# All four chunks run their second and third PV back to back, with LayerNorm of the next chunk ahead of the pair

## Chip, cores and metric

One core of a Trainium2 chip runs the kernel. The metric is the device time of one execution in microseconds (us); three executions of the kernel before took 562.66, 563.76 and 564.58 us, the median is 563.76. The engines are TensorE (PE), VectorE (DVE), ScalarE (ACT), GpSimd (POOL) and SyncE (SP), which here only issues transfers (DMA).

## What is computed

A transformer block whose two halves stand side by side on one normalised input: attention with 32 heads of 18 and a sliding window of 256 keys, and a gated feed-forward. The sequence is S = 2048, the width D = 576, the hidden width F = 4608, all in bf16.

```python
xn = _layernorm(x)                       # no weights
q, k, v = split(xn @ wqkv)               # 32 heads of 18
scores = einsum("bhqd,bhkd->bhqk", q, k) * 18 ** -0.5
p = softmax(where(0 <= i - j < 256, scores, -1e9))
attn = (p @ v) @ wo
ffn = (silu(xn @ w1) * (xn @ w3)) @ w2
return x + attn + ffn
```

## The kernel before

**Chunks and phases.** The sequence is cut into four chunks of 512 tokens (`c` = 0 to 3), each of four tiles of 128. A chunk has three phases on TensorE. First come the projections (L449; chunk 0 has its own ahead of the loop). Then follow 36 *units* (`u`, loop at L999): a unit is 128 columns of the hidden layer, nine pairs of matmuls of 64 rows each (`unit_pairs`, L701), one pair for gate and up each time; its tanh runs on ScalarE (`unit_tanh`, L710), its two multiplications on VectorE (`unit_h`, L716 and L719). The last phase, called P2 in the code, multiplies by W2 and Wo (L761, L767), adds the residual and stores.

**Attention between the units.** While the units run, attention is fed in between their matmul pairs. Heads go in eight groups of four (`g`). A *score step* (`scores` L575, `exps` L584, `masks` L611) makes one P tile; a group has four steps in chunk 0 and five in the others, so 32 and 40 steps a chunk. A *PV* (`pv`, L632) multiplies the P tiles of two groups by V: PV `j` takes groups 2j and 2j+1, so a chunk has four, of 72 small matmuls in chunk 0 and 96 in the others. PV 3 runs as P2 begins. PV 0 to 2 run among the units: each alone, after a unit (L1049), or two as a pair without anything between them, in the middle of a unit (L1009). `JOINT` says which two and where.

**After a PV.** VectorE moves the two PSUM banks of its result out (`pv_out`, L641) and takes a reciprocal (`o_scale`, L646), GpSimd scales (L647), VectorE turns the result back (`o_turn`, L654) into the buffer `od[j % 2]`, of which there are two, and transfers put its rows into `oT` (`o_pack` and `o_rest`, L658). `o_rest`, for the rows of PV 0 alone, is seven small transfers over the following units, on SP's queue, in chunk 0 on ScalarE's. A pair needs two more places for `pv_out`: they are P tiles that the pair has just read (`kept`).

**PSUM.** Eight banks: two for scores (`SC`), and three pairs (`JOBS`) which units and PVs take in turn. A unit can start only when VectorE has read what its pair held three jobs ago; a PV takes a pair like a unit does.

**P tiles.** They lie in ten buffers of their own (`pt`) and in memory that is free for a while: the last eight rows of `hT` (`h`), `stage` (`sh`), `od`, and the four W2 buffers (`w2`). `early` lists where the first steps' tiles go, `free` is the list from which later steps take, `held` keeps two for group 6, and `release` gives a PV's tiles back. A step waits in the order until a tile is to be had.

**The order** is written by the loop itself with a clock that counts matmul pairs: `last` says by when the steps should be done, and `spaced_step` spreads them over what remains, at least 7.5 pairs apart. A PV may run 20 pairs after its last step (`PV_AFTER`). Engines take their instructions in this order, SP its transfers too, each behind its waits.

**LayerNorm of the next chunk.** `near` gives for each of the next chunk's four tiles three units: one for the statistics (`ln_stats`, L357 to L360 on VectorE, L365 and L367 on GpSimd), one for the normalisation (`ln_apply`, L382 on VectorE) and one for the transfer that transposes it into `xnT` (`xn_send`, L407 on SP). The fourth tile has 34, 35 and 40 (the last one in P2). The tiles themselves come by `load_x` (L298): chunk 1's first two in unit 6 of chunk 0, the third in unit 8 and the fourth in unit 17 of each chunk. Weights of the units come in parts through SP (`load_part`, L322), W2 in pieces into a ring of four buffers (`load_w2`, L349), the first four of a chunk while its units still run.

Before, `JOINT` gave chunks 1 and 3 the pair of PV 1 and 2 in unit 27, and chunk 2 the pair of PV 0 and 1 in unit 18 with PV 2 alone after unit 25. Chunk 0 had no pair: its PVs ran after units 14, 20 and 27.

Of the kernel before, what the change touches and what calls it, by code (L numbers as in the profile page):

```python
# [164 lines left out]
def bass_parallel_sum__sliding_block__glu_gated_swiglu__prompt_kernel(  # L165
# [18 lines left out]
    NC = S // CH  # L184
# [13 lines left out]
    with ExitStack() as es:  # L198
# [143 lines left out]
        def load_w2(upto):  # L342
            nonlocal n2fill
            if n2fill >= min(upto, NC * 2 * NFC):
                return
            s = n2fill % NW2
            half, fc = divmod(n2fill % (2 * NFC), NFC)
            n2fill += 1
            add("sp", lambda e: e.dma_start(  # L349
                w2[s][:], B_w2[fc * 512:(fc + 1) * 512, half * HD:(half + 1) * HD].rearrange("(fl p) d -> p fl d", p=128)),  # L350
                w=[("w2", s)], dma=f"w2_{s}")
# [398 lines left out]
        def p2_item(c, item, xs):  # L750
            nonlocal of_ctr
            what, half, fc, k, tt, sl, last = item
            if what == "rest":
                wo_rest(half, False, k)
                return
            d0 = half * HD
            bank = PS[:, ACC[tt], 0:HD]
            key = [("ps", ACC[tt])]
            if what == "w2":
                f = fc * 4 + k  # L760
                add("pe", lambda e: e.matmul(  # L761
                    bank, hT[:, f, tt * 128:(tt + 1) * 128], w2[sl][:, k, :], start=(f == 0 and half == 1), stop=False),
                    r=[("h", f), ("w2", sl)], **{"w" if f == 0 and half == 1 else "j": key})
                if last:
                    load_w2((c + 1) * 2 * NFC + (2 if c + 1 < NC and JOINT[c + 1][0] == 0 else 0))
            elif what == "wo":
                add("pe", lambda e: e.matmul(  # L767
                    bank, oT[:, k, tt * 128:(tt + 1) * 128], wo[:, k, d0:d0 + HD], start=False, stop=(k == 3 and (half == 0 or c + 1 == NC))),
                    r=[("oT", j) for j in range(G // 2)] + ["wo"], j=key)
            else:  # L770
                o = of_ctr % NOF
                of_ctr += 1
                t = c * TB + tt
                add("dve", lambda e: e.tensor_tensor(ofin[:, o, :], bank, xp[xs[tt]][:, d0:d0 + HD], ALU.add),  # L774
                    r=key + [("xp", xs[tt])], w=[("of", o)])
                add("sp", lambda e: e.dma_start(out2[t * 128:(t + 1) * 128, d0:d0 + HD], ofin[:, o, :]),
                    r=[("of", o)], dma=f"out{o}")
# [132 lines left out]
        span_main(2, G, "act", slice(0, 2))  # L910

        PV_COST, PV_AFTER = 6.6, 20
        JOINT = {1: (1, 27, 7), 2: (0, 18, 4), 3: (1, 27, 8)}

        for c in range(NC):
            NS = len(steps_of(c))
            att = [(g, s) for g in range(G) for s in range(NS)]
            near = {0: (20, 22, 23), 1: (24, 26, 27), 2: (30, 32, 33), 3: (34, 35, 40)}
            plan = near if c + 1 < NC else {}
            stat, apply, xt = ({v[k]: i for i, v in plan.items()} for k in range(3))  # L920
            loads = {8: (2,), 17: (3,)} if c + 1 < NC else {}
# [3 lines left out]
            if c:  # L925
                total += 9 * sum(COST[kind] for kind, _ in PROJ)
            start = 60 if c == 0 else 42
            last = total - 24
            nxt = soon = start
            clock = 0.0  # L930
            done = 0
            pv_ready = {}
            free = [("pt", n) for n in range(NPT)]
            if c:
                free += [("sh", n) for n in range(4 if JOINT[c][0] == 0 else 2)]
            early = [("h", n) for n in range(4)]
            if c:
                early += [("w2", (c * 2 * NFC + n) % NW2) for n in range(2 if JOINT[c][0] == 0 else 0, 4)] + [("od", n) for n in range(NOD)]
            held = {} if c == 0 or JOINT[c][0] == 0 else {6 * NS: ("sh", 2), 6 * NS + 1: ("sh", 3)}
            side = {}  # L940
            jobs = {}
            next_pv = 0
# [1 line left out]
            def later(u, what):  # L944
                side.setdefault(u, []).append(what)

            def release(j, kept):
                for g in (2 * j, 2 * j + 1):
                    for st in range(NS):
                        sl = pt_of[(c, g, st)]  # L950
                        ok = ("pt", "sh", "h", "w2") if c and at_u < 22 and JOINT[c][0] == 1 else ("pt", "sh")
                        if sl[0] in ok:
                            (kept if kept is not None and len(kept) < 2 and sl[0] in ("pt", "sh") else free).append(sl)

# [44 lines left out]
            for u in range(NF):  # L999
# [6 lines left out]
                b0 = jobs[u] = job()  # L1006
                for n in range(9):
                    into = nxt - (clock + 9 - n)
                    if c and (u, n) == JOINT[c][1:]:  # L1009
                        ja = JOINT[c][0]  # L1010
                        assert next_pv == ja and ja + 1 in pv_ready and clock >= pv_ready[ja + 1], (c, next_pv, clock, pv_ready)
                        two = [job(), job()]
                        job_ctr += 1
                        kept = []
                        _DEBUG.setdefault("joint", []).append((c, u, n, done, round(clock - pv_ready[ja + 1], 1), len([o for o in P.ops if o.eng == "pe"])))
                        for m, j in enumerate((ja, ja + 1)):
                            pv(c, j, two[m])
                            clock += PV_COST
                            release(j, kept)
                        next_pv = ja + 2  # L1020
                        for m, sl in enumerate(kept):
                            uqs[2 + m:] = [pt_slot(sl).rearrange("p q r -> p (q r)").bitcast(dt.float32)]
                            uq_keys[2 + m:] = [pt_keys(sl)]
                        pv_out(two[0][0], 0)
                        pv_out(two[0][1], 1)
                        o_scale(0)
                        pv_out(two[1][0], 2)
                        pv_out(two[1][1], 3)
                        g = 2 * ja
                        later(u, lambda g=g: (o_turn(g, 0), o_turn(g, 1), o_scale(1)))  # L1030
                        later(u + 1, lambda g=g: o_turn(g + 1, 0))
                        later(u + 2, lambda g=g, ja=ja: (o_turn(g + 1, 1), o_pack(ja, "sp"), o_scale(2)))
                        later(u + 3, lambda g=g: (o_turn(g + 2, 0), o_turn(g + 2, 1), o_scale(3)))
                        later(u + 3, lambda kept=kept: free.extend(kept))
                        later(u + 4, lambda g=g: o_turn(g + 3, 0))
                        later(u + 5, lambda g=g, ja=ja: (o_turn(g + 3, 1), o_pack(ja + 1, "sp")))
                        if ja == 0:
                            for m in range(7):
                                later(u + 4 + m // 2 + m // 6, lambda m=m: o_rest(m, "sp"))
                    if done < len(att) and (free or done < len(early) or done in held) and (clock >= nxt or (n == 8 and into < 3 and clock >= soon)):  # L1040
                        spaced_step()
                    op = unit_pairs(c, u, n, n + 1, b0[0])
                    clock += 1
                    if n in (3, 8) or (n == 6 and c == 0 and u < 4):
                        owe_part(op)
                unit_tanh(u, b0[0])
                if u % 4 == 3 and u < NF - 8 and (c or u != 15):
                    owed += 6
                if (c == 0 or next_pv not in (JOINT[c][0], JOINT[c][0] + 1)) and next_pv in pv_ready and clock >= pv_ready[next_pv] and next_pv < 3:  # L1049
                    j = next_pv  # L1050
                    next_pv += 1
                    banks = job()
                    pv(c, j, banks)
                    clock += PV_COST
                    release(j, None)
                    later(u, lambda b=banks: (pv_out(b[0], 0), pv_out(b[1], 1), o_scale(0)))
                    later(u + 1, lambda j=j: (o_turn(2 * j, 0), o_turn(2 * j, 1), o_scale(1)))
                    later(u + 2, lambda j=j: o_turn(2 * j + 1, 0))
                    later(u + 3, lambda j=j: (o_turn(2 * j + 1, 1), o_pack(j, "sp")))
                    if j == 0:  # L1060
                        for n in range(7):
                            later(u + 4 + (n if c == 0 else n // 2 + n // 6), lambda n=n: o_rest(n, "sp" if c else "act"))
# [24 lines left out]
                if c == 0 and u == 28:  # L1087
# [3 lines left out]
                    for r in range(2):  # L1091
                        add("sp", lambda e, r=r: e.dma_start(
                            wo[64 * r:64 * r + 64, 4, :], head.rearrange("(t d) f -> t d f", d=Dh)[:, 0:16, :]), j=["wo"], dma="wo")
                if u in ((20, 22, 24, 26) if c == 0 else (JOINT[c][1] + 2, JOINT[c][1] + 6) if JOINT[c][0] == 0 else (27, 29, 31, 33)):
                    load_w2(c * 2 * NFC + 4)
                if u == 29:
                    xs = [load_x(c * TB + tt) for tt in range(TB)]
# [66 lines left out]
```

## Time and profile before

| | before |
|---|---|
| median of three runs | 563.76 us (562.66 to 564.58) |
| the profiled execution | 563.35 us |
| its span (first to last instruction) | 561.6 us |
| mean granted TensorE clock | 0.997 |
| PE busy / DVE busy / ACT busy / POOL busy | 554.8 / 309.3 / 259.4 / 163.1 us |

A group's row of the profile reads: line of the kernel, engine, operation, what it writes <- what it reads, shapes, count | busy time and mean of one | idle time of the engine before it, and what ended it. Rows of a time line begin with start and length in us; in brackets stands how long the engine was idle before and what released it. In the chain of waits (the chain of work that ended last) a row has start, length and what it was. "SPq" is SP's queue, where the length is the time the issues took. A busy PE is not PE at its peak: a matmul's end is modelled, and at half the granted clock it is busy for twice as long.

The costliest groups by line: the units' matmuls (L701) 184.0 and 153.4 us busy, W2's (L761) 146.6, the units' steps on VectorE 97.7 (L716) and 98.9 (L719), tanh (L710) 85.6, the exponentials (L584) 88.6, 24.4 and 18.4 by where they write.

### The profile page before, as it was taken

The page shows a single profiled execution, that of the slowest core. Times are in us where ns is not written, and L with a number is a line of the kernel's source. Part 1 is how long each engine was busy: PE and PEld are TensorE (multiplying, and loading weights), DVE is VectorE, ACT ScalarE, POOL GpSimd, SP SyncE. Part 2 cuts the span into 40 slices and gives each one's busy share as a digit, 9 for nine tenths or more (in the row PEclk, how much of TensorE's full clock was granted, in tenths as well). Part 3 has the DMA queues.
Part 4 walks back from the last instruction along what each step waited for, and adds up shares of the span by engine and source line. Part 5 has one row for each costly group of instructions (what it writes and reads, how often), then busy time and mean ns, then how long its engine had stood idle before and what let it go on. Part 6 is the DMA issues. An engine that isn't in the chain of part 4 may idle for free.

```text
span 561.6 us, 15732 instructions
## 1 busy us (share of the span) xinstructions
PE 554.8 (99%) x6766; PEld 333.1 (59%) x6766; DVE 309.3 (55%) x578; ACT 259.4 (46%) x357; POOL 163.1 (29%) x389
## 2 busy tenths in 40 slices
PE   8999999999999999999999999999999999999998
PEld 4445444777655455477764454447776554455776
DVE  6466889610466678841055668785105577678211
ACT  6457776000387775600057757640004767766000
POOL 6413454300033442530013325433000343333000
PEclk9999999999999999999999999989999999999999
DMA  9987889977266386666925853584572663634552
GB/s 241 215 164 184 201 152 205 172 192 193 72 140 158 97 207 142 173 167 172 225 60 135 182 167 89 132 200 112 151 203 54 138 171 97 173 109 124 141 148 64
DMA packets 127072, 85.96 MB, mean 153 GB/s; under 512 B 34179, under 2 KB 124763, under 8 KB 127003
## 3 DMA queue, kind: packets, MB, share of 16 engines
q1 hardware_dynamic: 125011, 82.69, 62.1%
q10 hardware_dynamic: 1992, 2.27, 1.7%
q8 instruction: 53, 0.87, 0.7%
q14 instruction: 16, 0.13, 0.1%
HBM read 71.29 MB, written 2.36 MB: 131 GB/s over the span
## 4 chain that ended last, share of the span: by engine, by line
PE 96%; DVE 2%; issue 1%; ACT 0%; DMA 0%; SPq 0%; POOL 0%; DVEq 0%
PE ps L701 48%; PE ps L761 25%; PE ps L449 9%; PE ps L575 6%; PE ps L632 3%; PE ps L767 3%; PE ps L796 1%; DVE gs L716 1%; DVE hT L719 1%; DVE od L654 0%; DMA oT<-od 0%; PE ps L687 0%; DVE xn L382 0%; PE ps L394 0%; ACT stage L829 0%
## 5 line engine op out<-in xcount | busy, mean ns | idle before, releaser
L701 PE MATMUL ps<-xnT,w 64*128 64x512 bf16 x1400 | 184.0, 377 | 2.1 <-DVE hT L719 2.1
L701 PE MATMUL ps<-xnS,w 64*128 64x512 bf16 x1120 | 153.4, 378 | 0.0
L761 PE MATMUL ps<-w,hT 128*128 128x288 bf16 x1152 | 146.6, 286 | 0.0
L716 DVE SCALAR_TENSOR_TENSOR gs<-th,ps 128x512 bf16<-128x512 bf16 x144 | 97.7, 678 | 81.6 <-ACT th L710 81.1
L761 PEld LDWEIGHTS ps<-w,hT 128*128 128x128 bf16 x1152 | 112.3, 98 | 29.0 <-issue 0.6
L584 ACT ACTIVATE pt<-ps 128x1024 bf16<-128x1024 f32 (+1 forms) x88 | 88.6, 1006 | 47.0 <-PE ps L575 46.6
L701 PEld LDWEIGHTS ps<-xnT,w 64*128 64x128 bf16 x1400 | 66.9, 94 | 68.0 <-DVE hT L719 2.6
L710 ACT ACTIVATE th<-ps 128x512 bf16<-128x512 f32 x144 | 85.6, 594 | 38.1 <-PE ps L701 35.3
L719 DVE SCALAR_TENSOR_TENSOR hT<-gs,ps 128x512 bf16<-128x512 bf16 x144 | 98.9, 687 | 5.0
L701 PEld LDWEIGHTS ps<-xnS,w 64*128 64x128 bf16 x1120 | 53.7, 94 | 52.3 <-issue 0.3
L774 DVE TENSOR_TENSOR ofin<-ps,xp 128x288 bf16<-128x288 f32 x32 | 13.8, 454 | 125.0 <-PE ps L767 66.9
L611 POOL TENSOR_TENSOR pt<-pt,mk 128x128 int32<-128x128 int32 (+1 forms) x156 | 63.1, 429 | 43.7 <-ACT pt L584 43.7
L462 ACT ACTIVATE stage<-ps 128x512 bf16<-128x512 f32 x16 | 9.5, 596 | 142.7 <-PE ps L449 140.4
L611 POOL TENSOR_TENSOR hT<-hT,mk 128x128 int32<-128x128 int32 (+1 forms) x45 | 18.3, 427 | 173.9 <-ACT hT L584 173.9
L575 PE MATMUL ps<-qv,kv 64*128 64x320 bf16 (+4 forms) x528 | 51.7, 261 | 0.0
L575 PEld LDWEIGHTS ps<-qv,kv 64*128 64x128 bf16 x528 | 25.5, 94 | 28.6 <-ACT hT L584 1.8
L449 PE MATMUL ps<-xnT,wp 64*128 64x512 bf16 (+1 forms) x360 | 37.9, 355 | 0.0
L654 DVE STREAM_TRANSPOSE od<-oq 128x256 bf16<-128x256 bf16 x64 | 25.8, 427 | 9.7 <-POOL oq L647 7.0
L449 PEld LDWEIGHTS ps<-xnT,wp 64*128 64x128 bf16 x360 | 18.7, 94 | 14.7
L584 ACT ACTIVATE hT<-ps 128x1024 bf16<-128x1024 f32 (+1 forms) x24 | 24.4, 1015 | 6.2 <-PE ps L575 5.9
L449 PE MATMUL ps<-wv,xnT 64*128 64x288 bf16 x288 | 22.2, 283 | 0.1
L584 ACT ACTIVATE w<-ps 128x1024 bf16<-128x1024 f32 x18 | 18.4, 1023 | 6.1 <-PE ps L575 5.9
(86 smaller groups left out, 375.6 us busy)
## 6 DMA issues: line engine op xcount, KB each, us to landing
w<-in_B_w_dram SPq DMA_DIRECT2D x208, 192.0 KB, 3.8
w<-in_B_w_dram SPq DMA_DIRECT2D x72, 288.0 KB, 3.3
xp<-in_A_x_dram SPq DMA_DIRECT2D x30, 144.0 KB, 3.0
out_dram<-ofin SPq DMA_DIRECT2D x32, 72.0 KB, 1.7
xnS<-xnT SPq DMA_DIRECT2D x8, 256.0 KB, 5.3
oT<-od SPq DMA_DIRECT2D x40, 36.0 KB
pt<-in_A_wqkv_dram SPq DMA_DIRECT2D x4, 288.0 KB, 6.4
hT<-in_B_w_dram SPq DMA_DIRECT2D x6, 192.0 KB, 3.6
```

What stands on the lines that cost most here:

```text
L449: op = add("pe", lambda e, out_=out_, st=st, mv=mv, n=n, r0=r0, first=first: e.matmul(out_, st, mv, start=first, stop=(part == 1 and n == ...
L575: add("pe", lambda e, r0=r0, out_=out_, kb=kb, q0=q0, nb=nb: e.matmul(out_, kb4[r0:r0 + 64, g, kb + NV - NB, :] if kb < 0 else kv[r0:r0 + ...
L584: add("act", lambda e: e.activation(pt_slot(sl)[:, 0:w, :], PS[:, SC[0]:SC[1] + 1, 0:w].rearrange("p r q -> p q r"), ACT.Exp, scale=scale) ...
L611: add("pool", lambda e, vb=vb, mm=mm: e.tensor_tensor(vb, vb, mm, ALU.mult), r=(key if n == 0 else []) + ["mk"], **{"w" if n == 0 else "j" ...
L632: add("pe", lambda e, p=p, q=q, pr=pr, sl=sl, g=g, pos=pos, q0=q0, nb=nb, col=col, first=first, n=n: e.matmul(PS[32 * q:32 * q + VW, banks ...
L654: add("dve", lambda e: e.transpose(od[i][:, g % 2, c0:c0 + CH // 2], oq[:, c0:c0 + CH // 2]), r=["oq", "oq0"], **{"j" if half or g % 2 els ...
L701: op = add("pe", lambda e, n=n, r0=r0, r=r, k=k, src=src: e.matmul(PS[:, b0 + r, :], wt[r0:r0 + 64, k, fl * 128:(fl + 1) * 128], src, star ...
L710: add("act", lambda e: e.activation(th[i][:], PS[:, bg, :], ACT.Tanh, scale=0.5), r=[("ps", bg)], w=[("th", i)])
L716: add("dve", lambda e: e.scalar_tensor_tensor(out=gs[i][:], in0=th[i][:], scalar=1.0, in1=PS[:, bg, :], op0=ALU.add, op1=ALU.mult), r=[("t ...
L719: add("dve", lambda e: e.scalar_tensor_tensor(out=hT[:, u, :], in0=gs[i][:], scalar=0.5, in1=PS[:, bu, :], op0=ALU.mult, op1=ALU.mult), r= ...
L761: add("pe", lambda e: e.matmul(bank, hT[:, f, tt * 128:(tt + 1) * 128], w2[sl][:, k, :], start=(f == 0 and half == 1), stop=False), r=[("h ...
L767: add("pe", lambda e: e.matmul(bank, oT[:, k, tt * 128:(tt + 1) * 128], wo[:, k, d0:d0 + HD], start=False, stop=(k == 3 and (half == 0 or ...
```

## The change

All four chunks now run PV 0 alone and PV 1 and 2 as a pair: in chunk 0 in unit 26 ahead of its last matmul pair, in chunk 1 in unit 27, in chunk 2 in unit 24 ahead of its fifth, in chunk 3 in unit 27. PV 0 of chunk 0 stands after unit 13 (before: 14), that of chunk 2 after unit 7. With `AHEAD`, the score steps of chunks 0 and 2 are to be done 16 matmul pairs sooner. LayerNorm of the next chunk's first three tiles is put by the pair's unit J: statistics in units J-13, J-9 and J-5, normalisation two units after each, the transfer one more.

All four W2 buffers now serve as early P tiles in every chunk, and `h` and `w2` tiles of PV 0 may be used again by the groups of PV 2. The first four W2 loads of a chunk stand in units J, J+2, J+4 and J+6; those two that came ahead of chunk 2 in the phase before are gone. Chunk 2's seven `o_rest` transfers now stand in units 11 to 15, with `o_pack` of PV 0 in unit 10. Chunk 0's `o_rest` stands in units 17 to 23 (before: 18 to 24).

```diff
-                    load_w2((c + 1) * 2 * NFC + (2 if c + 1 < NC and JOINT[c + 1][0] == 0 else 0))
+                    load_w2((c + 1) * 2 * NFC)
...
-        JOINT = {1: (1, 27, 7), 2: (0, 18, 4), 3: (1, 27, 8)}
+        JOINT = {0: (26, 8), 1: (27, 7), 2: (24, 4), 3: (27, 8)}
+        AHEAD = [40, 24, 40, 24]
...
-            near = {0: (20, 22, 23), 1: (24, 26, 27), 2: (30, 32, 33), 3: (34, 35, 40)}
+            near = {t: tuple(JOINT[c][0] - 13 + 4 * t + k for k in (0, 2, 3)) for t in range(3)} | {3: (34, 35, 40)}
...
-            last = total - 24
+            last = total - AHEAD[c]
...
             if c:
-                free += [("sh", n) for n in range(4 if JOINT[c][0] == 0 else 2)]
-            early = [("h", n) for n in range(4)]
+                free += [("sh", n) for n in range(4)]
+            held = {6 * NS + 1: free.pop(), 6 * NS: free.pop()}
+            early = [("h", n) for n in range(4)] + [("w2", (c * 2 * NFC + n) % NW2) for n in range(NW2)]
             if c:
-                early += [("w2", (c * 2 * NFC + n) % NW2) for n in range(2 if JOINT[c][0] == 0 else 0, 4)] + [("od", n) for n in range(NOD)]
-            held = {} if c == 0 or JOINT[c][0] == 0 else {6 * NS: ("sh", 2), 6 * NS + 1: ("sh", 3)}
+                early += [("od", n) for n in range(NOD)]
...
-                        ok = ("pt", "sh", "h", "w2") if c and at_u < 22 and JOINT[c][0] == 1 else ("pt", "sh")
+                        ok = ("pt", "sh", "h", "w2") if j == 0 else ("pt", "sh")
...
-                    if c and (u, n) == JOINT[c][1:]:
-                        ja = JOINT[c][0]
+                    if (u, n) == JOINT[c]:
+                        ja = 1
...
-                        if ja == 0:
-                            for m in range(7):
-                                later(u + 4 + m // 2 + m // 6, lambda m=m: o_rest(m, "sp"))
...
-                if (c == 0 or next_pv not in (JOINT[c][0], JOINT[c][0] + 1)) and next_pv in pv_ready and clock >= pv_ready[next_pv] and next_pv < 3:
+                if next_pv == 0 and next_pv in pv_ready and clock >= pv_ready[next_pv]:
...
-                if u in ((20, 22, 24, 26) if c == 0 else (JOINT[c][1] + 2, JOINT[c][1] + 6) if JOINT[c][0] == 0 else (27, 29, 31, 33)):
+                if u in range(JOINT[c][0], JOINT[c][0] + 7, 2):
                     load_w2(c * 2 * NFC + 4)
```

## The prediction

> **What bounds the kernel now.** I read the page first, then the same stage of the chunks side by side, then TensorE's waits, then the time lines around each wait. The page:
>
> ```profile
> span 561.6 us, 15732 instructions
> ...
> PE 554.8 (99%) x6766; PEld 333.1 (59%) x6766; DVE 309.3 (55%) x578; ACT 259.4 (46%) x357; POOL 163.1 (29%) x389
> ...
> PEclk9999999999999999999999999989999999999999
> ```
>
> TensorE (PE) works without a break and sets the end; its share of busy time hides how much of that is waiting between pieces or slow clock. One slice of 40 shows a lower granted clock. So the question is only where TensorE loses time that its own work does not need. The chunks 1, 2 and 3 do the same matmuls, so their stages can be laid against each other. Each row below runs from the chunk's first projection matmul to the first matmul of its W2 phase (columns: window, its length, then busy time and instructions of PE, of its weight loads, of DVE, ACT and POOL, then granted clock, DMA share, GB/s):
>
> ```profile
> 142.39:240.53 98.14, 97.76 (x1392) 51.19 (x1388) 70.12 (x130) 65.24 (x88) 35.58 (x86) 1.00 0.57 140
> 280.19:382.06 101.87, 99.72 (x1391) 52.29 (x1388) 70.96 (x130) 65.35 (x88) 35.58 (x86) 0.98 0.55 134
> 421.72:519.16 97.44, 97.44 (x1392) 53.63 (x1388) 65.88 (x113) 65.02 (x88) 33.01 (x78) 1.00 0.50 123
> ```
>
> The reader is to see that chunk 2 takes 101.87 us where chunk 1 takes 98.14 and chunk 3 97.44: some 4 us of chunk 2 are not work. TensorE's waits name most of it (total, times, longest):
>
> ```profile
> PE ps L701 <- DVE hT L719: 2.1, 1, 2.1
> ...
> PE ps L632 <- DVE hT L719: 0.4, 1, 0.4
> ```
>
> The first is in chunk 2, the second at the end of chunk 1. The first, in the rows of VectorE (DVE), of SyncE's queue (SP) and of TensorE:
>
> ```profile
> 359.84 0.69 DVE L719 SCALAR_TENSOR_TENSOR hT<-gs,ps 128x512 bf16<-128x512 bf16 x1
> 363.23 0.77 DVE L654 STREAM_TRANSPOSE od<-oq 128x256 bf16<-128x256 bf16 x2 [2.71 <-DMA oT<-od]
> ```
> ```profile
> 350.79 6.67 SPq L658 DMA_DIRECT2D oT<-od  x8
> ...
> 360.23 1.37 SPq L658 DMA_DIRECT2D oT<-od  x2
> ```
> ```profile
> 366.33 1.08 PE L701 MATMUL ps<-xnT,w 64*128 64x512 bf16 x8 [2.10 <-DVE hT L719]
> ```
>
> Chunk 2 runs PV 0 and 1 as the pair and PV 2 alone, after unit 25. PV 2's turn (L654) wants od buffer 0 again, and the last two transfers that read PV 0's rows from it were issued only at 360.23: SP had spent 6.67 us on eight such transfers. VectorE stands 2.71 us in front of its turn; the two hidden-unit steps queued behind it (L716, L719) free a PSUM pair late, and TensorE waits 2.10 us. What follows costs as much again:
>
> ```profile
> 363.85:366.33 2.48, 0.38 (x5) 0.01 (x2) 2.45 (x7) 1.39 (x2) 2.12 (x5) 1.00 0.96 265
> 366.33:368.07 1.74, 1.74 (x16) 0.88 (x18) 1.71 (x4) 0.00 (x0) 0.39 (x2) 0.75 1.49 195
> 368.07:370.62 2.55, 2.55 (x20) 0.92 (x15) 1.47 (x3) 1.62 (x2) 0.87 (x2) 0.50 0.92 192
> ```
>
> The granted clock is 0.75 for 1.74 us and 0.50 for 2.55 us, so 0.25 x 1.74 + 0.50 x 2.55 = 1.71 us are lost to the clock right behind the wait.
>
> **The change part by part.** No matmul, exponential, mask or transfer is added or taken away; only places change.
>
> Chunk 2: PV 0 alone after unit 7, the pair of PV 1 and 2 in unit 24. PV 0's transfers out of od buffer 0 are then put to SP in units 10 to 13, and PV 2's turn into it comes in unit 27, fourteen units later. Chunks 1 and 3 have had this arrangement all along, and the wait occurs once in the whole span:
>
> ```profile
> DVE od L654 <- DMA oT<-od: 2.7, 1, 2.7
> ```
>
> So I let chunk 2 fall to what its neighbours take. The floor is chunk 3 (97.44, without any LayerNorm), the ceiling chunk 1 less its own wait (98.14 - 0.38 = 97.76); in the middle 97.6, a gain of 4.27, between 4.11 and 4.43. Built from its parts it is 2.10 of wait, 1.71 of clock and a third one: chunk 2's pair. The chain of waits has the PVs so (start, length, what):
>
> ```profile
> 53.12 0.98 PE ps L632 x69
> ...
> 218.15 2.50 PE ps L632 x154
> ...
> 334.19 1.32 PE ps L632 x80
> 335.52 0.04 issue
> 335.56 1.36 PE ps L632 x87
> ...
> 353.95 1.30 PE ps L632 x89
> ```
>
> Chunk 2's pair takes 2.72 from 334.19, chunk 1's 2.50; the second PV there stands for a moment for the PSUM pair of the unit before. In unit 24 a score step stands in the unit ahead of it, which gives VectorE some 0.2 us more, so 0.22 goes: 2.10 + 1.71 + 0.22 = 4.03, the small rest being the restart after the wait. I take 4.27 from the stage, since it needs no list of parts.
>
> Chunk 1: its PE order hardly changes; LayerNorm of the next chunk's first three tiles goes ahead of the pair. The third tile's normalisation stood late, at the end of the chunk, in front of the last units' steps:
>
> ```profile
> 235.82 0.60 DVE L382 TENSOR_SCALAR xn<-xp,mv,rstd 128x576 bf16<-128x576 bf16 x2
> ```
> ```profile
> 239.11 0.32 PE L632 MATMUL ps<-stage,va 64*20 64x320 bf16 x4 [0.38 <-DVE hT L719]
> ```
>
> It (and the statistics ahead of it, over a microsecond together) moves to units 22 and 24, so VectorE reaches the last hidden step before TensorE asks: gain 0.38, between 0.2 and 0.44.
>
> Chunk 0: three single PVs become one single and a pair. In chunk 1 a pair takes 2.50 against 2 x 1.30 = 2.60, and a further entry is saved; for PVs of 0.98 I take a gain of 0.2, between 0 and 0.25. Against it stands a possible new wait. With the pair at the last matmul pair of unit 26, unit 27 needs the first PV's two PSUM banks moved out by VectorE. Chunk 3 has the same place (unit 27, last pair):
>
> ```profile
> 498.84 0.72 DVE L641 STREAM_TRANSPOSE uq<-ps 128x512 f32<-128x512 f32 x1 [0.98 <-PE ps L632]
> 499.48 0.67 DVE L641 STREAM_TRANSPOSE ofin<-ps 128x512 f32<-128x512 f32 x1
> ```
> ```profile
> 499.91 0.31 PE L575 MATMUL ps<-qv,kv 64*128 64x320 bf16 x2
> ```
>
> There the second move ends at 500.15 and TensorE, after a score step (0.22) and one matmul pair (0.22), comes to the next unit at 499.91 + 0.44 = 500.35: 0.20 to spare. Chunk 0's second PV is shorter by 1.30 - 0.98 = 0.32, so TensorE would come 0.12 us too early. I take a wait of 0.15, between 0 and 0.4 (the 0.38 above is the nearest such wait; the clock stayed at 1.00 behind it). Chunk 0 together: gain 0.05, between -0.4 and 0.25.
>
> Edits costed at nothing. The score steps of chunks 0 and 2 end 16 matmul pairs sooner: ScalarE (ACT) has the same exponentials to do, busy 65.35 of 101.87 us in chunk 2, and the smallest distance of two steps stays; if that cover went, each of the 72 steps would add its overhang. All four w2 buffers serve as P tiles in chunks 0 and 2, so their first W2 loads come later, in units 26 to 32 and 24 to 30. Chunk 1 loads them in units 27 to 33, its fourth only here:
>
> ```profile
> 240.40 0.58 SPq L349 DMA_DIRECT2D w<-in_B_w_dram  x1
> ```
>
> That is as the W2 phase begins (240.53), and no TensorE wait follows. The LayerNorm's transposing transfers pass the weight loads on SP; behind them stand parts of w13 that are wanted some six units later, and the x loads.
>
> Sum against the profiled execution (563.35 us for its span of 561.6): 563.35 - 4.27 - 0.38 - 0.05 = 558.65. The median of the runs, 563.76, lies 0.41 above this execution; from it the same sum gives 559.06. I take 558.8.
>
> **The rivals.**
>
> The slow stretch stays. If the lower clock did not hang on the wait, 1.71 of the gain is not had: 558.8 + 1.71 = 560.5. For it: a wait of 0.38 left chunk 1 at a clock of 1.00, so a short gap alone does not do it. Against: the only slow stretch in the span begins with the end of the longest wait. The Trainium skill, "TensorE: Matmul & The Clock Gate", section "HAM oscillation — how this bites in real kernels", has TensorE throttled again by idle gaps above some 3.4 us. By that rule a gap of 2.10 us would not have slowed it, and the time would be this rival's; the trace has 0.75 and 0.50 directly behind a gap of 2.10, so I give the row the word.
>
> The wait moves. A wait as long as chunk 2's appears elsewhere, most likely at chunk 0's od buffer 0 or where LayerNorm now shares VectorE with PV 0: 2.10 + 1.71 back, 562.6. For it: chunk 0 has the busiest queue on SP. Against: buffer 0 is left by unit 22 and wanted in unit 29, and chunk 0 has had PV 1 and a tile's statistics in one unit already, as the next rows show, with no wait of TensorE behind.
>
> Slower: the x load in chunk 0. The statistics of the next chunk's first tile move from unit 20 to unit 13. SP issues that tile's load late, VectorE takes its work in order, so a load that is not there stops the units' steps behind it:
>
> ```profile
> 49.75 0.95 SPq L298 DMA_DIRECT2D xp<-in_A_x_dram  x2
> ```
> ```profile
> 67.32 0.98 PE ps L632 x64
> ```
> ```profile
> 70.68 0.40 DVE L357 BATCH_NORM_STATS2 stats<-xp 128x6 f32<-128x288 bf16 x1
> ```
> ```profile
> DMA to landing us min/median/max: 2.2/3.0/7.6
> ```
>
> Before, the statistics start 3.4 us after PV 1 does. PV 0 moves up by a unit, about 1.9 us, and one score step, 0.2: from 53.12 to about 51.0, so they are due at 54.4. With the usual 2.2 to 3.0 us the tile is there by 52.8. With the longest landing, 7.6, it comes at 57.4: VectorE stands 3.0, TensorE by the ratio of chunk 2 (2.10 for 2.71) 2.3, and with 1.71 of clock the time is 562.8. It ends slower than before only if the tile lands after 60.8: then VectorE stands 6.4, TensorE 5.0, and with the clock the time is 565.5; at a landing of 12 us it would be 566.2. Nothing in front of that load on SP changes, so it needs a landing of over 11 us, which none of the 30 had.
>
> That the pairs do not form can be left out: the program's order has them.
>
> **How the numbers follow.** The forecast (chunk 2 like its neighbours, no new wait above half a microsecond) 0.76; slow stretch stays 0.06; the wait moves 0.10; slower by the x load or something unnamed of its size 0.08, of which 0.05 beyond 0.3%. Of this kernel's time a measurement can tell about 0.3%, 1.7 us, from no change: faster is below 562.1, slower above 565.5. Faster: 0.76 + 0.06 and half of the moved wait, 0.05, make 0.87; same 0.08; slower 0.05. The costs' bounds run from 4.11 + 0.2 - 0.4 = 3.9 to 4.43 + 0.44 + 0.25 = 5.1; taken off 563.35 and off 563.76 that is 558.2 to 559.9, and a run's own scatter (0.8 above the median, 1.1 below it) widens it downwards to 557.8. To hold 8 in 10 the upper end goes past the slow-stretch rival: 561.2.
>
> **What would show it.** Right: no DVE wait on a transfer out of od in the whole span; TensorE's list of waits without the 2.1 and the 0.4; the granted clock at 1.00 in all stages; the three windows of chunks 1, 2 and 3 within about 0.5 us of each other; chunk 2's pair at 2.5; chunk 0's pair at about 1.8, with at most 0.4 of wait behind it. Wrong: a TensorE wait above 1 us anywhere, above all in chunk 0's units 13 to 17 (the x tile) or around unit 29 (od); a slow stretch without a wait ahead of it; or chunk 2 still over 99 us with no wait in it, which would mean that its excess was not what I read.

## The result, and the profile after

The changed kernel takes 560.16 us (median of six runs, 559.73 to 560.96) where the kernel before took 563.90 beside it (six runs, 562.35 to 564.98): a ratio of 0.9938 with a 95% interval of 0.992 to 0.9956 (estimated from all runs of both, so not the quotient of the two medians). It is faster by 3.7 us, inside the range and about 1.4 us short of the 558.8 foretold. The profiled execution took 559.73 us. Its page:

```profile
span 558.0 us, 15733 instructions
...
PE 553.0 (99%) x6766; PEld 333.7 (60%) x6766; DVE 309.9 (56%) x578; ACT 259.4 (46%) x357; POOL 163.4 (29%) x389
...
PEclk9999999999999999999999999999999999999999
```

The slice with the lower clock is gone, and a busy share of 99% looks as it did before. TensorE's waits (total, times, longest):

```profile
PE ps L796 <- DVE oq L791: 1.2, 1, 1.2
PE ps L761 <- DMA w<-in_B_w_dram: 0.7, 1, 0.7
```

The waits of 2.1 and 0.4 for VectorE are gone. The first row, of the warm-up, stood there before as well. The second is new: a W2 matmul waits for its weights. The stages by windows, cut where the chain of waits has the matmuls, as in the prediction (window, length, busy times, clock, DMA share, GB/s); the first is chunk 0 from its first unit to its first W2 matmul, the second chunk 0's W2 phase, then chunks 1 and 2 from the first projection to the first W2 matmul:

```profile
21.78:102.95 81.17, 81.17 (x1086) 40.43 (x1082) 62.37 (x115) 52.17 (x71) 28.40 (x69) 1.00 0.87 176
...
102.95:143.52 40.57, 39.83 (x326) 31.38 (x328) 6.89 (x17) 0.00 (x0) 4.90 (x12) 1.00 0.80 191
143.52:241.16 97.64, 97.64 (x1391) 51.89 (x1388) 70.66 (x130) 65.56 (x88) 35.71 (x86) 1.00 0.60 142
280.82:378.45 97.63, 97.63 (x1391) 51.92 (x1388) 70.69 (x130) 65.57 (x88) 35.64 (x86) 1.00 0.65 145
```

Before, chunk 0 had these two:

```profile
21.66:102.73 81.07, 81.07 (x1085) 39.87 (x1082) 62.15 (x115) 52.57 (x71) 28.30 (x69) 1.00 0.90 183
```
```profile
102.73:142.39 39.66, 39.66 (x327) 31.47 (x328) 6.88 (x17) 0.00 (x0) 4.88 (x12) 1.00 0.82 182
```

So between the two profiled executions (563.35 and 559.73, 3.62 apart) chunk 2 gave 101.87 - 97.63 = 4.24 us and chunk 1 98.14 - 97.64 = 0.50; chunk 0 took back 0.10 in its units and 40.57 - 39.66 = 0.91 in its W2 phase, and the start was 0.12 later, which is scatter (in five executions of the kernel before it differs by up to 0.5). Chunk 3 kept its 97.44. That is 3.61 in all. What took the 0.91 is seen in SP's queue, in the chain of waits and on TensorE:

```profile
97.04 2.02 SPq L298 DMA_DIRECT2D xp<-in_A_x_dram  x4
99.11 1.25 SPq L322 DMA_DIRECT2D w<-in_B_w_dram  x2
100.40 0.60 SPq L349 DMA_DIRECT2D w<-in_B_w_dram  x1
101.05 3.12 SPq L658 DMA_DIRECT2D oT<-od  x4
104.21 3.16 SPq L349 DMA_DIRECT2D w<-in_B_w_dram  x3
```
```profile
100.40 7.26 DMA w<-in_B_w_dram
107.67 0.05 issue
107.71 1.40 PE ps L761 x10
```
```profile
107.71 1.52 PE L761 MATMUL ps<-w,hT 128*128 128x288 bf16 x11 [0.74 <-DMA w<-in_B_w_dram]
```

The third of chunk 0's first four W2 loads stands in unit 30. SP, which works its list in order, comes to it at 100.40, behind the pair's `oT` rows, the Wo and x loads and weight parts. The transfer then takes 7.26 us to land, with the DMA engines busier over these 7.26 us (share 1.13) than in the chunk's units (0.87):

```profile
100.40:107.66 7.26, 6.58 (x121) 4.42 (x115) 6.11 (x14) 0.60 (x2) 4.26 (x11) 1.00 1.13 217
```

The W2 phase began at 102.95 and has used up its first two pieces when TensorE begins to wait, at 107.71 - 0.74 = 106.97. The fourth load, in unit 32, is issued at 104.21 with the next ones.

### The profile page after: what moved, and what is told of

The parts are those of the page before. It is cut to its first block, busy times and chain, and to the rows that moved or that the text cites. A ratio compares the mean times of both kernels' runs of the same rounds, so it can differ in the third digit from the quotient of the medians.

```text
span 558.0 us, 15733 instructions
## 1 busy us (share of the span) xinstructions
PE 553.0 (99%) x6766; PEld 333.7 (60%) x6766; DVE 309.9 (56%) x578; ACT 259.4 (46%) x357; POOL 163.4 (29%) x389
## 4 chain that ended last, share of the span: by engine, by line
PE 97%; DMA 1%; ACT 0%; DVE 0%; SPq 0%; issue 0%; POOL 0%
PE ps L701 50%; PE ps L761 25%; PE ps L449 9%; PE ps L575 6%; PE ps L632 3%; PE ps L767 3%; DMA w<-in_B_w_dram 1%; PE ps L796 1%; PE ps L687 0%; PE ps L394 0%; ACT stage L829 0%; ACT xnT L401 0%; SPq L322 0%; DVE ofin L774 0%; DVE xn L374 0%
## 5 line engine op out<-in xcount | busy, mean ns | idle before, releaser
L701 PE MATMUL ps<-xnT,w 64*128 64x512 bf16 x1400 | 186.0, 376 | 0.0
L584 ACT ACTIVATE pt<-ps 128x1024 bf16<-128x1024 f32 (+1 forms) x70 | 70.8, 1011 | 39.0 <-PE ps L575 38.8
L611 POOL TENSOR_TENSOR hT<-hT,mk 128x128 int32<-128x128 int32 (+1 forms) x59 | 24.1, 430 | 176.3 <-ACT hT L584 176.2
L611 POOL TENSOR_TENSOR pt<-pt,mk 128x128 int32<-128x128 int32 (+1 forms) x124 | 50.2, 430 | 29.3 <-ACT pt L584 29.1
L584 ACT ACTIVATE w<-ps 128x1024 bf16<-128x1024 f32 (+1 forms) x32 | 32.3, 1010 | 11.8 <-PE ps L575 11.7
L584 ACT ACTIVATE hT<-ps 128x1024 bf16<-128x1024 f32 (+1 forms) x32 | 32.3, 1010 | 6.6 <-PE ps L575 6.2
L611 POOL TENSOR_TENSOR w<-w,mk 128x128 int32<-128x128 int32 (+1 forms) x56 | 22.8, 429 | 28.2 <-ACT w L584 28.2
```

What stands on the lines that cost most here:

```text
L584: add("act", lambda e: e.activation(pt_slot(sl)[:, 0:w, :], PS[:, SC[0]:SC[1] + 1, 0:w].rearrange("p r q -> p q r"), ACT.Exp, scale=scale) ...
L611: add("pool", lambda e, vb=vb, mm=mm: e.tensor_tensor(vb, vb, mm, ALU.mult), r=(key if n == 0 else []) + ["mk"], **{"w" if n == 0 else "j" ...
L701: op = add("pe", lambda e, n=n, r0=r0, r=r, k=k, src=src: e.matmul(PS[:, b0 + r, :], wt[r0:r0 + 64, k, fl * 128:(fl + 1) * 128], src, star ...
```

## The experiments

The ratios are against the kernel before, run beside each. The windows in this section begin and end at a matmul's own start in TensorE's rows, up to 0.2 us ahead of where the chain has it. So measured, the change's four stages (chunk 0's units and W2 phase, chunks 1 and 2) are:

```profile
21.62:102.88 81.26, 81.26 (x1088) 40.46 (x1083) 62.46 (x115) 52.27 (x71) 28.36 (x68) 1.00 0.87 176
102.88:143.35 40.47, 39.73 (x335) 31.36 (x326) 6.87 (x16) 0.00 (x0) 4.93 (x12) 1.00 0.80 192
143.35:241.09 97.74, 97.74 (x1394) 51.91 (x1389) 70.68 (x130) 65.56 (x88) 35.64 (x86) 1.00 0.60 141
280.65:378.38 97.73, 97.73 (x1394) 51.95 (x1388) 70.71 (x130) 65.57 (x88) 35.59 (x85) 1.00 0.65 145
```

Those of the kernel before are 81.17, 39.56, 98.23 and 101.98.

**The W2 loads alone.** Chunk 0's four loads are put directly behind the pair:

```diff
-                if u in range(JOINT[c][0], JOINT[c][0] + 7, 2):
-                    load_w2(c * 2 * NFC + 4)
+                if u in (range(JOINT[c][0], JOINT[c][0] + 7, 2) if c else (26, 27)):
+                    for _ in range(1 if c else 2):
+                        load_w2(c * 2 * NFC + 4)
```

> The changed kernel with one difference: chunk 0's four W2 loads go to SP in units 26 and 27, two each, directly behind the pair, ahead of the oT, Wo and x transfers (instead of units 26, 28, 30, 32). My theory: TensorE's wait of 0.74 us at 107.7 us comes from SP's queue, which issues the third W2 load only at 100.40. Then the wait goes, chunk 0's W2 phase (first W2 matmul to chunk 1's first projection) falls from about 40.6 us to about 39.7, and the time falls by about 0.9 us, to a ratio of about 0.9920 to 0.9925 against the kernel before. Rival: the transfers themselves are slow there because the DMA engines are full (7.26 us from issue to landing); then another load, the last of the four or a w13 part, is late in its place, TensorE waits as long, and the time stays at 0.9938.

Measured: 558.89 us (six runs, 558.67 to 560.55), ratio 0.9916 (0.9893 to 0.9939). SP issues the four in one go, and the W2 phase is back at the 39.56 it had before:

```profile
85.23 3.02 SPq L349 DMA_DIRECT2D w<-in_B_w_dram  x4
```
```profile
104.50:144.06 39.56, 39.56 (x332) 31.40 (x326) 6.82 (x16) 0.00 (x0) 4.90 (x12) 1.00 0.75 173
```

No other load became late: TensorE waits for no DMA in this run. So an earlier place in SP's queue is enough to end the wait. It was not the whole cause, though. From its issue at 100.40 the third load had 6.57 us until TensorE asked for it at 106.97, and such loads of the changed kernel land after 3.3 us in the median, so with a usual landing it would have been there (an estimate from these figures). Late issue and slow landing made the wait together. The profiled execution, at 560.55 the longest of the six, has something else in chunk 0's units, 82.83 us against 81.26:

```profile
PE ps L701 <- issue: 1.0, 2, 0.8
```

That is TensorE waiting with no releaser that the profile shows; such a wait comes up again below.

**LayerNorm back in its old units,** the rest of the change kept:

```diff
-            near = {t: tuple(JOINT[c][0] - 13 + 4 * t + k for k in (0, 2, 3)) for t in range(3)} | {3: (34, 35, 40)}
+            near = {0: (20, 22, 23), 1: (24, 26, 27), 2: (30, 32, 33), 3: (34, 35, 40)}
```

> The changed kernel with LayerNorm's units put back to where the kernel before had them (20/22/23, 24/26/27, 30/32/33). My theory: the move ahead is worth chunk 1's wait of 0.38 and nothing else, so chunk 1's stage (first projection to first W2 matmul) goes from 97.64 back to about 98.1; chunks 0 and 2, whose pairs stand in units 26 and 24 with the late tile in units 30 to 32, get a wait of 0 to 0.4 each. The time rises by 0.4 to 1.2 us against the changed kernel, ratio 0.9945 to 0.996. Rival: LayerNorm collides with the four moves behind the pair; then a wait of over 1 us with a slow stretch appears in chunk 0 or 2 and the time rises by 2 us or more.

Measured: 561.54 us, ratio 0.9963 (0.9948 to 0.9979), so 0.0025 of the time, 1.4 us, above the change. Waits of TensorE, and the windows of chunk 0's W2 phase, chunk 1 and chunk 2:

```profile
PE ps L761 <- DMA w<-in_B_w_dram: 1.4, 1, 1.4
PE ps L796 <- DVE oq L791: 1.2, 1, 1.2
PE ps L632 <- DVE hT L719: 0.6, 2, 0.4
```
```profile
103.17:144.32 41.15, 39.73 (x334) 31.34 (x326) 6.86 (x16) 0.00 (x0) 4.92 (x12) 1.00 0.83 197
144.32:242.49 98.17, 97.78 (x1394) 51.18 (x1389) 70.16 (x130) 65.22 (x88) 35.40 (x86) 1.00 0.57 140
282.05:379.98 97.93, 97.93 (x1395) 51.77 (x1389) 70.46 (x130) 65.00 (x88) 35.59 (x85) 1.00 0.58 138
```

Chunk 1's wait is back and costs 0.43 us (98.17 against 97.74) as expected; chunk 2 loses 0.20, and chunk 0's units 0.23 (81.49 against 81.26). What I had not named, and what takes the rise above the 1.2 us expected: the W2 phase of chunk 0 loses another 0.68 us (41.15 against 40.47). SP's list has a transposing transfer between the first and the third W2 load now:

```profile
87.83 1.22 SPq L407 DMA_TRANSPOSE xnT<-xn  x1
...
101.32 0.60 SPq L349 DMA_DIRECT2D w<-in_B_w_dram  x1
```

The third load is issued 1.85 us ahead of the W2 phase (101.32 to 103.17), in the changed kernel 2.48 (100.40 to 102.88). So the move is also worth something on SP; that this transfer is what delayed the load is read from the list, not tried by itself.

**The od buffer's wait alone.** The kernel before, with the seven small transfers of chunk 2 moved from SP to ScalarE and a unit sooner:

```diff
-                                later(u + 4 + m // 2 + m // 6, lambda m=m: o_rest(m, "sp"))
+                                later(u + 3 + m // 2 + m // 6, lambda m=m: o_rest(m, "act"))
```

> The kernel before with one difference: in chunk 2 PV 0's seven small transfers out of od buffer 0 are issued by ScalarE one unit sooner instead of by SP; the pair of PV 0 and 1 and everything else stays. My theory: VectorE's wait of 2.71 us for that buffer is SP's lateness, TensorE's wait of 2.10 follows from it and the slow clock from that wait. Then all three go (DVE's wait under 0.5, no TensorE wait in chunk 2, clock 1.00), chunk 2's stage falls from 101.87 to about 98.0, the time by 3.5 to 3.9 us: ratio 0.993 to 0.994. Rival (slow clock has another cause): the stage falls by 2.1 to 2.3 only, the clock stays low around 366 to 370 us, ratio 0.996.

Measured: 561.82 us, ratio 0.9961 (0.9947 to 0.9976). VectorE's wait for a transfer out of od is gone, so is TensorE's of 2.10 behind it, and the clock is 1.00 in all of chunk 2. Its stage falls less than expected, from 101.98 to 99.39 where 98.0 was expected, and another wait came in:

```profile
281.29:380.68 99.39, 98.57 (x1395) 52.41 (x1389) 71.12 (x130) 65.11 (x88) 35.58 (x85) 1.00 0.59 137
```
```profile
347.31 1.23 ACTq L658 DMA_DIRECT2D oT<-od  x2
```
```profile
349.66 0.39 PE L575 MATMUL ps<-qv,kv 64*128 64x320 bf16 x6 [0.76 <-ACT pt L584]
```

Issuing two transfers held ScalarE for 1.23 us, the exponentials came late and TensorE waited 0.76 for the score banks. That is 0.76 of the missing 1.4 us; the rest has no wait to its name. The ratio is the one that the rival gave, but not for the rival's reason: the granted clock is 1.000 in all ten runs, where 19 of the 29 runs of the kernel before beside them have 0.996 or 0.997. The direction holds: the od wait is real, it is the lateness of these transfers on SP, and it can be removed without touching the pair (engine and unit were changed together, so which of the two did it is not told apart). With the wait the lowered clock goes too. The pair's move does it without a wait of its own.

**Chunk 2's pair alone.** The kernel before with chunk 2 like chunk 1:

```diff
-        JOINT = {1: (1, 27, 7), 2: (0, 18, 4), 3: (1, 27, 8)}
+        JOINT = {1: (1, 27, 7), 2: (1, 27, 7), 3: (1, 27, 8)}
```

> The kernel before with chunk 2 alone changed: its pair is PV 1 and 2 in unit 27 as in chunk 1, PV 0 alone; LayerNorm, chunk 0 and the rest stay. My theory: the gain of the change is chunk 2's alone, 101.87 to about 98.1 (chunk 1's figure with LayerNorm late), so the time falls by 3.6 to 3.9 us: ratio 0.993 to 0.994, as good as the whole change. Rival: chunk 2 needs LayerNorm out of the way as well; then a new wait stands at its end and the ratio is 0.995 or more.

Measured: 561.96 us, ratio 0.9966 (0.9947 to 0.9984). Chunk 2's window and TensorE's waits:

```profile
280.15:380.40 100.25, 97.96 (x1395) 52.03 (x1389) 70.33 (x130) 65.22 (x88) 35.42 (x86) 1.00 0.56 137
```
```profile
PE ps L632 <- issue: 1.9, 1, 1.9
...
PE ps L632 <- DVE hT L719: 0.8, 2, 0.4
```

The od wait is gone here too, and without the 1.90 the stage would be 98.35, close to what was expected, with the late LayerNorm's 0.38 now at the end of chunk 2 as well. The ratio is on the rival's side (0.995 or more), and the rival's wait is there, but it is the smaller part. The 1.90, in the middle of the pair, has no releaser in the profile, and the times (561.13 to 563.81 over ten runs) leave hardly any room for executions without it: 561.79, the profiled one, less 1.90 would be 559.9. What it is stays open. One of the ten, the longest, has a lowered clock (0.997).

**Making VectorE late on purpose.** The changed kernel, with one half of PV 2's turn in chunk 2 made eight and twelve times more (`m` is 8 or 12):

```diff
-                        later(u + 3, lambda g=g: (o_turn(g + 2, 0), o_turn(g + 2, 1), o_scale(3)))
+                        later(u + 3, lambda g=g, m=8 if c == 2 else 0: (o_turn(g + 2, 0), [o_turn(g + 2, 0) for _ in range(m)], o_turn(g + 2, 1), o_scale(3)))
```

> The changed kernel with one difference: in chunk 2's unit 27 VectorE makes the first half of PV 2's turn (L654) eight times more, about 0.37 us each, 3.0 us in all; the result is the same. TensorE has some 0.8 us to spare there, so it should wait about 2.1 us in one piece, as long as in the kernel before. My theory (a wait of that length brings the slow stretch): the granted clock falls to 0.75 and 0.50 behind it, chunk 2's stage grows by 2.1 + 1.7 = 3.8 us to about 101.5. Rival (the slow stretch is not the wait's): the clock stays at 1.00 and the stage grows by 2.1 to 2.3 only, to 99.9.

> As the run with eight more turns, with twelve: VectorE late by 4.4 us, TensorE's wait about 3.6 us. My theory: the same slow stretch of some 1.7 us, perhaps longer, so chunk 2's stage at 97.7 + 3.6 + 1.7 = 103.0 or above. Rival: 101.4 with the clock at 1.00.

Measured: 561.88 us with eight (0.9978, 0.996 to 0.9996) and 565.48 with twelve (1.0032, 1.0016 to 1.0047). TensorE's wait, chunk 2's window and the stretch behind the wait, first for eight:

```profile
368.25 0.39 PE L701 MATMUL ps<-xnT,w 64*128 64x512 bf16 x2 [1.58 <-DVE hT L719]
```
```profile
280.36:379.85 99.49, 97.91 (x1394) 51.96 (x1389) 73.91 (x138) 65.67 (x88) 35.51 (x85) 1.00 0.64 142
368.25:372.50 4.25, 4.25 (x42) 2.06 (x44) 4.15 (x8) 1.62 (x2) 2.21 (x6) 1.00 0.68 152
```

then for twelve:

```profile
370.86 0.39 PE L701 MATMUL ps<-xnT,w 64*128 64x512 bf16 x2 [3.49 <-DVE hT L719]
```
```profile
281.05:384.14 103.09, 99.60 (x1394) 52.47 (x1388) 75.79 (x142) 65.68 (x88) 35.54 (x85) 0.98 0.62 137
370.86:374.50 3.64, 3.64 (x22) 1.50 (x24) 3.18 (x6) 1.02 (x1) 2.23 (x6) 0.54 0.16 35
```

A wait of 3.49 us brings the slow stretch: the clock is 0.54 for 3.64 us, 1.7 us lost, and the stage is where my theory had it (103.0). Seven of the ten runs have a granted clock of 0.994 to 0.997, the other three 1.000. A wait of 1.58 brings none, in none of ten runs. It is shorter than I meant although each turn took 0.48 us and not 0.37: TensorE had some 2.3 us to spare (8 x 0.48 - 1.58), not 0.8. So a wait can cause the stretch; whether one of 2.1 always does was still open.

**The kernel before, looked at four times more.**

> The kernel before once more, for a second look at the same wait. My theory: VectorE's wait for the od buffer and TensorE's behind it come again within half a microsecond (2.7 and 2.1). If the slow stretch follows from every such wait it is there again with about 1.7 us; if it depends on something that differs from execution to execution it is longer, shorter or absent, and chunk 2's stage is then between 100.2 and 102.5.

> The kernel before, a third execution with a profile. Its many times so far lie in two groups, 561.9 to 562.9 and 563.8 to 565.4 us. My theory: the wait of 2.1 to 2.6 us in chunk 2 comes in every execution and the slow stretch behind it in some; a profiled execution above 563.2 us has the stretch (chunk 2's stage about 102), one below has a stage of 100.2 to 100.8 with the clock at 1.00. Rival: the groups have another cause, such as TensorE waits without a releaser in other places, and the stage does not go with the time.

> The kernel before, a fourth execution with a profile; the theories and their numbers are those of the third.

> The kernel before, a fifth execution with a profile; the theories and their numbers are those of the third.

Measured, with the first profiled execution of the kernel before ahead:

| execution | time | chunk 2's stage | TensorE's wait in it | clock of the stage | most of the wait inside one step of the clock |
|---|---|---|---|---|---|
| shown in the prediction | 563.35 | 101.98 | 2.10 | 0.98 | 2.10 |
| second | 563.09 | 100.78 | 2.58 | 1.00 | 1.55 |
| third | 562.00 | 100.45 | 2.24 | 1.00 | no change of clock to count from |
| fourth | 563.61 | 102.18 | 2.39 | 0.98 | 2.26 |
| fifth | 562.63 | 100.41 | 2.22 | 1.00 | 1.13 |

The wait comes every time, the slow stretch in two of five. The stage goes with the time in all five, and the last three, which were measured after the line of 563.2 us was drawn, fall on the side that was foretold. That the clock is behind the two groups of times is settled by the other runs, each of which has its granted clock on record. Of the 23 runs of the kernel before beside the turns, the 13 at 561.9 to 562.9 us have 0.999 or 1.000, the ten at 563.8 to 565.4 have 0.996 or 0.997. Beside the first four experiments the two lie less cleanly apart: two of the ten with a full clock took 564.1 and 564.2. Of all 53 beside the experiments 29 have the lowered clock. The six kernels whose longest TensorE wait in the profile is under 1.6 us have it in none of 48 runs: the change, the early loads, LayerNorm back, the od wait alone, eight turns and the last version below.

The last column says what decides, as far as these traces go. The clock they record changes in steps of 3.413 us: in the first execution it is full for 361.81 us (from 5.39 to 367.20), half for 3.41 and full again for 191.15 (370.61 to 561.76), and the two full stretches are 106 and 56 such steps. Counted from each execution's own changes of the clock, these are the steps around the wait, first in the fourth execution and then in the second, whose only change is at the very end:

```profile
363.09:366.50 3.41, 1.15 (x14) 0.38 (x8) 2.95 (x8) 1.69 (x3) 2.00 (x5) 1.00 0.98 259
366.50:369.92 3.42, 3.30 (x20) 1.34 (x22) 3.29 (x7) 0.55 (x2) 0.51 (x2) 0.50 1.11 203
```
```profile
363.18:366.59 3.41, 1.86 (x20) 0.74 (x16) 2.07 (x6) 1.85 (x3) 1.08 (x2) 1.00 0.70 191
366.59:370.01 3.42, 2.39 (x26) 1.17 (x28) 3.35 (x7) 1.47 (x2) 1.42 (x5) 1.00 1.19 213
370.01:373.42 3.41, 3.41 (x40) 1.74 (x38) 3.31 (x8) 2.65 (x5) 1.05 (x3) 1.00 0.67 133
```

In the fourth, TensorE is idle for 3.41 - 1.15 = 2.26 us of one step, and the whole next step runs at 0.50. In the second a longer wait lies across the edge of two steps, 1.55 and 1.03, and the clock stays at 1.00. With twelve turns it is 3.14 in one step, followed by one at half clock; with eight turns 1.53 and in chunk 2's pair alone 0.99, followed by none. So a step with 2.10 us or more of idle time was followed by a slow one and a step with 1.55 or less was not; where between the limit lies, these runs do not show.

**Both together.** The early W2 loads, and chunk 0's pair two matmul pairs sooner (shown against the changed kernel; the loads are as above):

```diff
-        JOINT = {0: (26, 8), 1: (27, 7), 2: (24, 4), 3: (27, 8)}
+        JOINT = {0: (26, 6), 1: (27, 7), 2: (24, 4), 3: (27, 8)}
```

> The run with early W2 loads in chunk 0, and chunk 0's pair two matmul pairs sooner in unit 26 (ahead of the seventh instead of the ninth). My theory: unit 27 no longer meets the moves of the first PV's banks; chunk 0's stage from its first unit to its first W2 matmul falls from 81.26 to about 81.0, its W2 phase stays at 39.56, and the whole takes about 558.5 us, ratio 0.991, the fastest of all. Rival: the pair was not what made chunk 0's stage longer than its 81.17 before; then the stage stays at 81.2 to 81.3.

Measured: 559.12 us (six runs, 558.38 to 559.67), ratio 0.992 (0.9901 to 0.9939). Chunk 0's units and its W2 phase:

```profile
21.78:102.70 80.92, 80.92 (x1089) 40.07 (x1083) 62.58 (x115) 52.65 (x71) 28.60 (x69) 1.00 0.83 187
102.70:142.26 39.56, 39.56 (x334) 31.44 (x326) 6.86 (x16) 0.00 (x0) 4.93 (x12) 1.00 0.73 173
```

The stage falls by 81.26 - 80.92 = 0.34 us, more than the 0.13 by which it differs among the change and its two versions with turns (81.13 to 81.26), where these units are the same; the W2 wait is gone. It is not the fastest of all, as was expected: the early loads alone took 558.89. Both versions with early loads have medians below the change's 560.16, but the intervals of the three overlap; it is the windows that show what was won.

## Why the prediction was right, and where it was off

**Chunk 2: right in place and mechanism; the clock was one execution's.** The stage was put at 97.6 and is 97.63. The pair came out at 2.46 us (2.5 foretold) and no DVE wait on a transfer out of od is left. The run with the od wait alone undone shows that TensorE's wait hangs on VectorE's and the lowered clock on that wait, and the twelve turns bring both back. But the 1.71 us of slow clock, taken as a fixed term, are there in two of five profiled executions and in 29 of 53 other runs. Against an execution without them the stage gives 100.4 to 100.8 less 97.73, some 2.7 to 3.1 us, and not 4.27. That the execution from which the sum was made had the stretch was chance. The 0.75 of the prediction is a mean over a stretch of 1.00 and one of 0.50: the half clock begins 0.87 us behind the wait and lasts 3.41, which costs the same 1.71. Of the 4.24 the wait, the clock and the pair (2.72 to 2.46) are 4.07; the rest was called the restart, and no row shows what it is. PV 0's small transfers end in unit 15 and not in 13 as the prediction has it, still twelve units ahead of PV 2's turn.

**Chunk 1: right.** Foretold 97.76, measured 97.64. With LayerNorm back it is 0.43 longer, so the 0.4 to 0.5 is the move's.

**Chunk 0's pair: right to 0.2 us.** The pair takes 1.85 (foretold about 1.8); the chain of waits has it and chunk 2's so:

```profile
80.59 1.85 PE ps L632 x122
...
350.12 2.46 PE ps L632 x168
```

Gain and new wait were set against each other at 0.2 and 0.15 in favour; it is 0.10 the other way (81.07 to 81.17), which is within the scatter of these units. The meeting with the banks' moves is there, though the list of waits does not name it:

```profile
82.32 0.67 DVE L641 STREAM_TRANSPOSE ofin<-ps 128x512 f32<-128x512 f32 x1
```
```profile
82.80 0.64 PE L701 MATMUL ps<-xnT,w 64*128 64x512 bf16 x3
```

The second move ends at 82.99. The two matmuls that open unit 27 start together elsewhere; here the first starts at 82.80, and the next only at 83.05 (the row ends at 83.44, and one takes 0.39). So the price is 0.25 rather than 0.15. With the pair two matmul pairs sooner the stage is 80.92 against 81.17 before, so the pair without that price is worth up to 0.25.

**The W2 loads: wrong.** This is the step that failed. They were costed at nothing, with chunk 1 as the precedent: loads in units 27 to 33, the fourth issued as the W2 phase begins, no wait behind. Chunk 0 is not like chunk 1 there. It has three Wo transfers more in unit 28, and its third load landed late, after 7.26 us, where the prediction reckoned with chunk 1's lateness alone. The price was 0.91 us of the profiled execution (waits of 0.74, 0.51 and 1.11 in this and the two runs with extra turns), and it was outside the bounds of every edit. The run with the loads moved shows it to be all of chunk 0's loss in the W2 phase. With the measured terms in place of the forecast ones, 563.35 - 4.24 - 0.50 + 0.10 + 0.91 + 0.12 = 559.74, and the profiled execution took 559.73; this closes because the stages fill the span, and is no test of the causes. It took 1.08 more than the forecast sum of 558.65, and the W2 loads are 0.91 of that.

**The rivals.** The slow stretch stays: false; no profiled execution without a wait of over 2 us has one, none of the change's six runs has a lowered clock, and a longer wait brought it back. The wait moves: in kind it did, to the W2 loads and with a quarter of the size, though not to od or LayerNorm, where I looked for it. Slower by the x load: the tile was there when VectorE asked, at 54.80 us (54.4 foretold); VectorE waits for an x tile only at the very start, 0.4 us, and the longest landing of an x load was 5.7 us.

## What to carry to other kernels

When a load is moved later, take its price from the queue it stands in, at that place: count the issue time of everything ahead of it, and use landing times from the same stretch, not from another with fewer transfers. Lay equal stages side by side before looking at waits; the difference of two windows finds stalls that a busy share of 99% hides, and checks a sum after the change. A loss that depends on the clock should be read from several executions, or from the granted clock of many runs, before it is put into a sum.

## What the runs showed of the hardware

TensorE's clock can fall behind a single wait of 2.1 to 2.4 us, to half for one step of 3.41 us, which costs 1.71 us, nearly as much as the wait; but waits of 2.22, 2.24 and 2.58 us in the same place passed without it, as did 1.58 and 1.90, and one of 3.49 had it. What tells them apart, in the seven of these eight whose steps can be counted, is how much idle time fell into one step: 2.10, 2.26 and 3.14 us against 1.55 at most. The Trainium skill, "TensorE: Matmul & The Clock Gate", section "What's actually happening", describes the activity window of some 3.4 us as free-running. That would let the same wait fall well or badly, and the trace agrees: its steps are 3.41 us long and lie differently over the same wait from execution to execution. The slow cases behind 2.10 and 2.39 us are below the idle time that the page's section on oscillation names.

TensorE also waits, in some kernels and places, up to 1.90 us with no releaser in the profile. That was not tried further.
